# An attention and routed-experts kernel: later loads for step 5, a small table built in three steps, and contiguous one-hots for the large one

## The chip, the cores and the metric

The kernel runs on one core of one Trainium2 chip. The metric is the device time of one execution in microseconds; the time before is 355.25 us, the median of 4 runs (354.03 to 358.31). The engines are named as the profile names them: PE does matrix products (PEld loads their weights), DVE and ACT work element by element, POOL does small work and issues most of the transfers, and SP issues the others.

## The reference

Two layers follow each other. The first is attention with normalized queries and keys; the second sends each token to one of eight experts, by a hash of its token id.

```
q, k, v: (8 batches, 12 heads, 448 tokens, 64)
q_n, k_n = q / rms(q) * g_q, k / rms(k) * g_k          # over the last axis
attn = softmax(q_n @ k_n^T / 8)
x = (attn @ v), transposed to (3584 tokens, 768)
expert = token_ids * 2654435761 % 8
for e in range(8):                                     # w1: (8, 768, 1024), w2: (8, 1024, 768)
    rows = tokens with expert == e
    out[rows] = relu(x[rows] @ w1[e]) @ w2[e]
```

## The kernel before

**Attention** works in 48 steps, each for two heads of a batch that lie six apart; six steps make a batch. A step has these parts: square queries and keys (`prep_sq`, on DVE, or on ACT for the groups in `ACT_SQ`), sum the squares on PE against a unit matrix (`prep_sum`) and finish the sum on DVE (`prep_red`); logarithm and exponential on ACT give the reciprocal root (`prep_ln`, `prep_er`); normalize on DVE (`prep_norm`); transpose on PE and copy out on DVE (`transpose`, `evacuate`); four score products on PE (`score`), four exponentials on ACT (`expo`), the product with the values on PE (`av_part`, in three parts), and the scaling by the row sums on DVE (`row_sums`, `put_x`). The results go to `x_scratch` in DRAM, a batch at a time.

The order is written out by hand: `emit` takes a text of tokens such as `sqk:1.0` (square the keys of group 1), and each engine executes its instructions strictly in the order in which they were emitted. One text covers the setup and the first twelve steps, a second, `steady`, is repeated for batches 2 to 7. `spin:n` emits n matmuls of zeros that keep PE busy. The first steps are loaded singly: step 0 and step 5 (`HP - 1`) from SP and ACT as fp32, the pairs 1 to 2 and 3 to 4 from POOL. The loads of step 5 are issued by SP right behind those of step 0 and of the token ids; the slots of its tiles that no load fills are zeroed by DVE (`zero`, part 3).

**The small table** lists, for experts 0 and 1, which token sits in which slot, so that their rows can be gathered while attention still runs. It is made in pieces between attention steps: small DVE operations stand in `SIDE`, matmuls with a follow-up on DVE in `AV_SIDE`, by the step in which they are placed. The matmuls write into columns of the bank of `av_ps` that attention leaves free; `m13a` does 28 of them at once, one for each column of 128 tokens, in step 31, `m13b` scales the result by -32768 and 1, and `m14a` adds the two halves with a unit matrix (`rep4`) in step 34.

**Experts** work on PE without a break: `gemm1` (48 matmuls, then Relu on ACT or DVE) and `gemm2` for each of four tiles of 128 rows, whose result is copied out by ACT (even tiles) or DVE (odd tiles) and scattered by POOL. Before each tile, `turn` transposes one gathered tile of a later expert on PE into the one bank of `ps_x`, and DVE copies it out. `before` and `between` say which tile is turned where.

**The large table**, for all experts from 2 on, is made while expert 0 runs. `plan` puts its parts behind a group of `gemm1` ("g") or a tile of `gemm2` ("k"). `p3` to `p11` compute each token's slot and split it into a high and a low digit (`hl`). `low` and `high` compare the digits with the numbers 0, 1, 2, ... and so make one-hots; `high_tok` multiplies the high ones by the token number, and `table_mm` takes 28 products of 128 x 56 over them. `fetch(2, ...)` then gathers expert 2's rows. The one-hots are laid out with the digit outside and the 28 columns inside; for that, `numbers` spreads the numbers over a tile `num` on ACT, in four parts.

Of the kernel before, what the change touches and what calls it, by code (L numbers as in the profile page):

```python
# [20 lines left out]
def kernel(  # L21
# [12 lines left out]
    nc = tc.nc  # L34
# [75 lines left out]
    rep4 = consts.tile([P, LO0], FP16)  # L110
# [49 lines left out]
    def setup3():  # L160
# [15 lines left out]
        for g in range(NL):  # L176
            r = slice(LO0 * g, LO0 * g + LO0)
            G.tensor_copy(rep4[r], ident16[r, r])
# [74 lines left out]
    with tc.manual_schedule(), \  # L253
# [96 lines left out]
        ACT_SQ = ((0, 1), (1, 1), (3, 1), (5, 0))  # L350
# [100 lines left out]
        comb = rt([P, 2, 2 * HI0], FP16, "comb")  # L451
# [63 lines left out]
        def m11(e):  # L515
            h = slice(HI0 * e, HI0 * e + HI0)
            V.tensor_tensor(out=hi[:, 1, h], in0=hi[:, 0, h], in1=wide(tv16, HI0), op=ALU.mult)
# [6 lines left out]
        def m13a(av):  # L524
            for c in range(NTC):
                g = LO0 * (c % NL)
                nc.tensor.matmul(av[g:g + LO0, SP:SP + 4 * HI0], lhsT=lo[:, :, c],
                                 rhs=hi[:, :, :, c], start=False, stop=(c >= NTC - NL),
                                 skip_group_check=True)

        def m13b(av):
            for a in range(2):
                o = SP + 2 * HI0 * a
                V.tensor_scalar_mul(comb[:, a], av[:, o:o + 2 * HI0], 1.0 if a else -32768.0)

        def m14a(av):
            for a in range(2):
                nc.tensor.matmul(av[0:LO0, SP:SP + 2 * HI0], lhsT=rep4[:], rhs=comb[:, a],
                                 start=False, stop=(a == 1), skip_group_check=True)
# [10 lines left out]

        def n1():
            V.memset(ones_e[:], 1.0)
# [169 lines left out]
        def zero(part):  # L722
# [11 lines left out]
            elif part == 3:  # L734
                zero_kv(V, raw(1, HP - 1)[:, None])
                zero_q(V, raw(0, HP - 1))
# [11 lines left out]
        load_one(HP - 1)  # L748
# [24 lines left out]
        AV_SIDE = {17: (m5a, m5b), 19: (m7a, m7b), 31: (m13a, m13b), 34: (m14a, m14b)}  # L773
        SIDE = {4: (m1, m2, m3), 5: (m4,), 7: (m8, m9), 11: (n1, n2), 12: (m15,), 13: (n3,),
# [46 lines left out]
        def emit(text, b):  # L821
# [18 lines left out]
            zero:1 zero:6 zero:0 gain:0 sqk:0.0 zero:2 spin:12 sumk:0.0 sqq:0.0 zero:7  # L840
            spin:2 sumq:0.0 redk:0.0 ln:0.1.2 er:0.1.2 redq:0.0 nk:0 ln:0.0.1 zero:3
            spin:3 Tk:0 er:0.0.1 sqk:1.0 spin:1 sumk:1.0 nq:0 sqq:1.0 Tq:0 redk:1.0 kT:0
            sumq:1.0 redq:1.0 qT:0 ln:1 v:1 spin:2 sc:0.0 er:1 nk:1 nq:1 sc:0.1 exp:0.0
            spin:2 Tk:1 kT:1 sc:0.2 kT:2 v:0 sc:0.3 sqk:2.0.0 exp:0.1 exp:0.2 spin:1
            Tq:1 qT:1 av:0.0 qT:2 sc:1.0 exp:0.3 sqk:2.0.1 sc:1.1 sc:1.2 sqq:2.0.0
            sumk:2.0 av:0.1 sqq:2.0.1 exp:1.0 sc:1.3 exp:1.1 redk:2.0 exp:1.2 v:2
            sumq:2.0 redq:2.0 av:0.2 sc:2.0 exp:1.3 ln:2 er:2 sc:2.1 rec:0 sc:2.2 x:0
            exp:2.0 nk:3 av:1.0 nq:3 Tk:3 kT:3 sc:2.3 av:1.1 av:1.2 exp:2.1 kT:4 nk:5
            Tq:3 rec:1 exp:2.2 qT:3 exp:2.3 qT:4 sc:3.0 nq:5 sc:3.1 sqk:3.0 sqq:3.0
            sumk:3.0 redk:3.0 exp:3.0 sc:3.2 exp:3.1 sumq:3.0 sc:3.3 exp:3.2 x:1 av:2.0  # L850
            redq:3.0 ln:3 sqk:4.0 Tk:5 Tq:5 sc:4.0 sc:4.1 exp:3.3 sqq:4.0 av:2.1 er:3
            av:2.2 kT:5 qT:5 sc:4.2 nk:6 exp:4.0 Tk:6 exp:4.1 exp:4.2 sc:4.3 exp:4.3
            sc:5.0 rec:2 x:2 av:3.0 kT:6 kT:7 av:3.1 sumk:4.0 sc:5.1 sc:5.2 nq:6 v:3
            exp:5.0 exp:5.1 redk:4.0 exp:5.2 Tq:6 sqk:4.1 av:3.2 sc:5.3 qT:6 qT:7 rec:3
            x:3 sc:6.0 sumq:4.0 exp:5.3 sc:6.1 sc:6.2 redq:4.0 sumk:4.1 exp:6.0 sqq:4.1
            av:4.0 redk:4.1 sqk:5.0 sc:6.3 sumq:4.1 exp:6.1 exp:6.2 av:4.1 redq:4.1 ln:4
            av:4.2 sc:7.0 sc:7.1 exp:6.3 er:4 sumk:5.0 v:4 rec:4 x:4 nk:8 redk:5.0
            av:5.0 Tk:8 nq:8 kT:8 exp:7.0 av:5.1 kT:9 av:5.2 rec:5 sqq:5.0 x:5 sc:7.2
            sumq:5.0 sc:7.3 exp:7.1 redq:5.0 av:6.0 exp:7.2 Tq:8 av:6.1 av:6.2 exp:7.3
            nk:10 qT:8 sc:8.0 sqq:5.1 sc:8.1 qT:9 exp:8.0 rec:6 x:6 sc:8.2 exp:8.1  # L860
            sumq:5.1 av:7.0 sc:8.3 nq:10 redq:5.1 exp:8.2 Tk:10 sqk:5.1 kT:10 av:7.1
            av:7.2 sc:9.0 exp:8.3 exp:9.0 kT:11 sc:9.1 rec:7 x:7 sc:9.2 Tq:10 exp:9.1
            av:8.0 v:5 qT:10 qT:11 sc:9.3 av:8.1 sumk:5.1 sqq:6.0 exp:9.2 redk:5.1
            exp:9.3 ln:5 av:8.2 er:5 rec:8 sc:10.0 sc:10.1 sc:10.2 x:8 sumq:6.0 exp:10.0
            av:9.0 av:9.1 exp:10.1 nk:14 nk:12 redq:6.0 av:9.2 sc:10.3 nq:12 rec:9 Tk:12
            exp:10.2 x:9 exp:10.3 sc:11.0 sc:11.1 av:10.0 kT:12 kT:13 exp:11.0 av:10.1
            sqq:6.1 Tq:12 qT:12 exp:11.1 sc:11.2 av:10.2 qT:13 rec:10 sc:11.3 nq:14
            exp:11.2 sc:12.0 x:10 sumq:6.1 exp:11.3 exp:12.0 redq:6.1
# [26 lines left out]
    with tc.manual_schedule(), \  # L895
# [108 lines left out]
        num = m_rt.tile([P, P, NTC], FP16)  # L1004
        lo1 = m_rt.tile([P, P, NTC], FP16)
        hi1 = m_rt.tile([P, NHI - HB, NTC], FP16)
# [74 lines left out]
        def numbers(part):  # L1081
            r = slice(32 * part, 32 * part + 32)
            nc.scalar.copy(num[:, r], iota_h[:, r, None].to_broadcast([P, 32, NTC]))
            if part == 3:
                nc.scalar.copy(tvh[:], tv[:])

        def low(part):
            r = slice(32 * part, 32 * part + 32)
            V.tensor_tensor(out=lo1[:, r], in0=num[:, r],
                            in1=hl[:, 1, None, :].to_broadcast([P, 32, NTC]), op=ALU.is_equal)  # L1090

        def high():
            V.tensor_tensor(out=hi1[:], in0=num[:, HB:NHI],
                            in1=hl[:, 0, None, :].to_broadcast([P, NHI - HB, NTC]),
                            op=ALU.is_equal)

        def high_tok():
            V.tensor_tensor(out=hi1[:], in0=hi1[:],
                            in1=tvh[:, None, :].to_broadcast([P, NHI - HB, NTC]), op=ALU.mult)

        def table_mm():
            val = ps_h.tile([P, 512], FP32, name="h_ps")[:, 0:NHI - HB]
            for c in range(NTC):
                nc.tensor.matmul(val, lhsT=lo1[:, :, c], rhs=hi1[:, :, c],
                                 start=(c == 0), stop=(c == NTC - 1))
# [19 lines left out]
        def each(f, *parts):  # L1125
# [3 lines left out]
            (0, "g", 0): each(numbers, 0), (0, "g", 1): [p3] + each(numbers, 1),  # L1129
            (0, "g", 2): [p4, p5] + each(numbers, 2), (0, "g", 3): [p6] + each(numbers, 3),  # L1130
            (0, "g", 4): [p7, p8], (0, "g", 5): [p9, p10, p11],
            (0, "g", 6): each(low, 0, 1), (0, "g", 7): each(low, 2, 3) + [high],
            (0, "k", 0): [high_tok], (0, "k", 1): [table_mm, lambda: fetch(2, range(KT))],
# [89 lines left out]
```

## Time and profile before

| | us |
|---|---|
| median of 4 runs | 355.25 |
| the profiled execution | 356.22 |
| its span, first to last instruction | 354.6 |
| ACT's first square / first exponential | 6.04 / 15.63 |
| matmuls of the small table, step 31 | 119.42 to 121.28 |
| first product of expert 0 | 169.89 |
| matmuls of the large table | 185.00 to 187.86 |
| last scatter | 348.87 |

A row of the timeline gives the start, the length, the engine, the line of the kernel, the operation with its output and input, and how often it stands there; in square brackets stands how long the engine was idle before it, and what ended the wait. A row of the busy times by stage gives a stretch, its length and the busy time of each engine in it.

### The profile page before, as it was taken

The numbers are of one execution on the slowest core, as the hardware profiler recorded it, in microseconds if no ns is written. First come the engines' busy times: TensorE is split into PE (matmuls) and PEld (weight loads), VectorE is DVE, ScalarE is ACT, GpSimd is POOL, SyncE is SP. The second block draws the span as 40 slices with busy tenths as digits, with TensorE's granted clock in tenths as the row PEclk, the third lists the DMA queues.
The fourth block names the chain that finished last, engine by engine and source line by source line (L and its number), as shares of the span: only waits on it lengthen the run. The fifth ranks groups of instructions, "written<-read, shape, count | busy, mean of one in ns | idle before, by whom it ended". The sixth has DMA issues, their size and how long they took to land. (4 is left out here: it accounts for less than half of the span.)

```text
span 354.6 us, 9268 instructions
## 1 busy us (share of the span) xinstructions
PE 335.6 (95%) x3894; PEld 235.2 (66%) x3894; DVE 202.9 (57%) x486; ACT 190.5 (54%) x289; POOL 146.6 (41%) x202
## 2 busy tenths in 40 slices
PE   5989999999999999997999999999999999999992
PEld 2466776766677777664867767767676676766751
DVE  2799999999999799773672243232232233223210
ACT  2499999999999899997722221212111111211210
POOL 8789926325420100012565455736456461303122
PEclk9699999999999999998999999999999999999997
DMA  6999999999999998032589999999999995203012
GB/s 85 209 202 205 199 236 200 238 202 219 203 248 211 252 209 194 3 79 68 130 171 203 272 276 239 258 250 236 260 220 267 228 232 186 112 0 125 24 71 90
DMA packets 41659, 64.82 MB, mean 183 GB/s; under 512 B 9743, under 2 KB 29655, under 8 KB 41232
## 3 DMA queue, kind: packets, MB, share of 16 engines
q0 software_dynamic: 37856, 58.10, 81.8%
q1 hardware_dynamic: 3456, 5.90, 5.4%
q8 instruction: 31, 0.51, 0.5%
q10 hardware_dynamic: 304, 0.21, 0.2%
q14 instruction: 12, 0.10, 0.1%
HBM read 89.29 MB, written 17.30 MB: 301 GB/s over the span
## 5 line engine op out<-in xcount | busy, mean ns | idle before, releaser
L632 ACT ACTIVATE expT<-sc_ps 128x896 bf16<-128x896 f32 x144 | 123.5, 935 | 5.7 <-PE sc_ps L616 5.1
L928 PEld LDWEIGHTS <-h_sb 128*128 128x128 f16 (+1 forms) x512 | 51.2, 104 | 30.5 <-ACT h_sb L915 0.5
L941 POOL DMA_INDIRECT out_dram<-o_sb,gidx x32 | 32.5, 1017 | 83.9 <-ACT o_sb L938 55.0
L928 PE MATMUL o_ps<-w_sb,h_sb 128*128 128x512 f16 (+3 forms) x384 | 66.2, 326 | 0.0
L915 ACT ACTIVATE h_sb<-h_ps 128x480 f16<-128x480 f32 (+2 forms) x44 | 21.7, 498 | 68.7 <-PE h_ps L911 61.9
L911 PEld LDWEIGHTS <-w_sb 128*128 128x128 f16 x336 | 44.5, 146 | 15.6 <-issue 1.2
L220 POOL DMA_INDIRECT kr<-x_scratch,gidx x32 | 32.7, 1022 | 48.0 <-DVE srec L673 37.1
L938 ACT COPY o_sb<-o_ps 128x768 f32<-128x768 f32 x16 | 12.8, 799 | 69.8 <-PE o_ps L928 57.3
L911 PE MATMUL h_ps<-xT,w_sb 128*128 128x480 f16 x240 | 49.4, 366 | 0.0
L650 PE MATMUL av_ps<-v,expT 128*128 128x65 bf16 x864 | 46.0, 194 | 3.0 <-DVE x_sb L681 2.9
L650 PEld LDWEIGHTS <-expT 128*128 128x128 bf16 x864 | 39.4, 98 | 14.0 <-DVE x_sb L681 8.6
L616 PE MATMUL sc_ps<-qT,kT 64*128 64x448 f16 x288 | 44.3, 361 | 1.5 <-DVE qT L608 0.6
L917 DVE TENSOR_SCALAR h_sb<-h_ps 128x480 f16<-128x480 f32 x28 | 18.4, 658 | 47.2 <-PE h_ps L911 47.2
L938 DVE COPY o_sb<-o_ps 128x768 f32<-128x768 f32 (+1 forms) x15 | 14.3, 956 | 33.6 <-PE o_ps L928 33.6
L232 DVE COPY xT<-xT_ps 128x768 f16<-128x768 f16 x28 | 15.5, 553 | 28.7 <-PE xT_ps L231 28.7
L294 POOL DMA_DIRECT2D vr<-in_v_dram x36 | 23.8, 671 | 17.0 <-DMA kr<-in_k_dram 6.2
L681 DVE TENSOR_TENSOR x_sb<-av_ps,srec 128x448 f16<-128x448 f32 x48 | 29.9, 623 | 1.4
L376 PEld LDWEIGHTS <-ident 128*128 128x128 f16 x576 | 23.2, 100 | 10.7 <-issue 5.7
L635 ACT ACTIVATE expT<-sc_ps 128x448 bf16<-128x448 f32 x48 | 27.6, 575 | 0.0
L655 PE MATMUL av_ps<-v,expT 128*128 128x130 bf16 x144 | 25.3, 222 | 0.0
L605 DVE TENSOR_SCALAR kT<-qkT_ps,g_col 128x512 f16<-128x512 f16 x48 | 21.0, 478 | 2.7 <-PE qkT_ps L576 2.5
L928 PE MATMUL o_ps<-kr,h_sb 128*128 128x512 f16 (+3 forms) x128 | 22.1, 326 | 0.0
(202 smaller groups left out, 452.0 us busy)
## 6 DMA issues: line engine op xcount, KB each, us to landing
w_sb<-in_moe_w_dram POOLq DMA_DIRECT2D x18, 512.0 KB
w_sb<-in_moe_w_dram POOLq DMA_DIRECT2D x8, 768.0 KB
kr<-in_k_dram POOLq DMA_DIRECT2D x7, 672.0 KB
qr<-in_q_dram POOLq DMA_DIRECT2D x7, 672.0 KB
x_scratch<-x_sb SPq DMA_DIRECT2D x15, 288.0 KB, 6.7
w_sb<-in_moe_w_dram POOLq DMA_DIRECT2D x2, 1536.0 KB
qr<-in_moe_w_dram POOLq DMA_DIRECT2D x6, 512.0 KB
vr<-in_v_dram POOLq DMA_DIRECT2D x14, 192.0 KB
```

The lines of the kernel that those rows point to most:

```text
L220: nc.gpsimd.indirect_dma_start(out=xg[0:idx.shape[0], :], out_offset=None, in_=x_dram[0:rows, :], in_offset=bass.IndirectOffsetOnAxis(ap=i ...
L294: eng.dma_start(out=dst[64 * half:64 * half + 64, :, s0:s0 + cnt, :].rearrange("p n s d -> p n (s d)"), in_=runs(t, h0 + HP * hh, 1, n, to ...
L616: nc.tensor.matmul(sc[:, hh, :S], lhsT=kT[64 * hh:64 * hh + 64, P * j:P * j + P], rhs=qT[64 * hh:64 * hh + 64, :], start=True, stop=True)
L632: nc.scalar.activation(expT[:, 2 * j:2 * j + 2, :], sc[:, :, :S], AF.Exp, bias=0.0, scale=1.0)
L635: nc.scalar.activation(expT[:, 6, :], sc[:, 0, :S], AF.Exp, bias=0.0, scale=1.0)
L650: nc.tensor.matmul(av[:, 2 * t + hh, :], lhsT=expT[:, tl(hh, j), P * t:P * t + P], rhs=v8[:, i, vs(hh, j), 0:D + 1], start=(hh == 0 and t ...
L655: nc.tensor.matmul(av[:, 2 * t:2 * t + 2, :], lhsT=expT[:, 6, P * t:P * t + P], rhs=v8[:, i, 0::7, 0:D + 1], start=False, stop=False)
L681: nc.vector.tensor_tensor(out=xs[b][:, :, hp * D:hp * D + D], in0=av[:, :, :D], in1=srec[:, :, None].to_broadcast([P, SL, D]), op=ALU.mult)
L911: nc.tensor.matmul(h_ps[:, :c1 - c0], lhsT=w1v[:, co, fo, :], rhs=xT[:, co, c0:c1], start=(co == 0), stop=(co == CO - 1))
L928: nc.tensor.matmul(o_ps[d0 > 0][0:w, d0:d1], lhsT=h_sb[:, fo, col * P:col * P + w], rhs=w2_sb[:, fo, d0:d1], start=(fo == 0), stop=(fo == ...
L938: (nc.vector.tensor_copy if col % 2 else nc.scalar.copy)(o_sb[0:w], o_ps[0][0:w])
L941: scat = nc.gpsimd.indirect_dma_start(out=out[:, :], out_offset=bass.IndirectOffsetOnAxis(ap=idx[0:w], axis=0), in_=o_sb[0:w], in_offset=N ...
```

## The change

Four things change together.

1. **The first steps.** Step 5's loads are no longer emitted at once: `zero` part 3 now emits two ACT copies of zeros into the free slots and the loads behind them, and the order text has it behind the first squares. The square of group 3's keys is no longer in `ACT_SQ`, and goes to DVE. The whole text of the first steps is another one.
2. **The small table.** Its matmuls are split over steps 31, 32 and 33 (10, 10 and 8). Each part is copied out by itself; the scaling by -32768 and 1 moves into the matrix `rep`, so `m14a` does six small matmuls, in step 35. The product of the high one-hots with the token number (`m11`) goes from DVE to POOL. `m15` and `n3` swap places, and `ones_e` is filled by POOL in the setup.
3. **The large table.** The one-hots are laid out with the columns outside and the digit inside, so that the operands of each matmul are contiguous; `numbers` and its tile go. `one_hot` compares the row of numbers, repeated for each column, with each column's digit, repeated for each number.
4. **The plan of expert 0.** `high`, `high_tok`, `table_mm` and `fetch(2)` each stand one tile later; two turned tiles swap places.

```diff
-    rep4 = consts.tile([P, LO0], FP16)
+    rep = consts.tile([P, 2, LO0], FP16)
...
-            G.tensor_copy(rep4[r], ident16[r, r])
+            for a, one in enumerate((-32768.0, 1.0)):
+                G.tensor_scalar(out=rep[r, a], in0=ident16[r, r], scalar1=one, scalar2=None,
+                                op0=ALU.mult)
+        G.memset(ones_e[:], 1.0)
...
-        ACT_SQ = ((0, 1), (1, 1), (3, 1), (5, 0))
+        ACT_SQ = ((0, 1), (1, 1), (5, 0))
...
-        comb = rt([P, 2, 2 * HI0], FP16, "comb")
+        PIECES = 3
+        comb = rt([P, PIECES, 2, 2 * HI0], FP16, "comb")
...
         def m11(e):
             h = slice(HI0 * e, HI0 * e + HI0)
-            V.tensor_tensor(out=hi[:, 1, h], in0=hi[:, 0, h], in1=wide(tv16, HI0), op=ALU.mult)
+            nc.gpsimd.tensor_tensor(out=hi[:, 1, h], in0=hi[:, 0, h], in1=wide(tv16, HI0), op=ALU.mult)
...
-        def m13a(av):
-            for c in range(NTC):
+        def m13a(av, i):
+            c1 = min(10 * i + 10, NTC)
+            for c in range(10 * i, c1):
...
-        def m13b(av):
-            for a in range(2):
-                o = SP + 2 * HI0 * a
-                V.tensor_scalar_mul(comb[:, a], av[:, o:o + 2 * HI0], 1.0 if a else -32768.0)
+        def m13b(av, i):
+            V.tensor_copy(comb[:, i].rearrange("p a h -> p (a h)"), av[:, SP:SP + 4 * HI0])
 
         def m14a(av):
-            for a in range(2):
-                nc.tensor.matmul(av[0:LO0, SP:SP + 2 * HI0], lhsT=rep4[:], rhs=comb[:, a],
-                                 start=False, stop=(a == 1), skip_group_check=True)
+            for i in range(PIECES):
+                for a in range(2):
+                    nc.tensor.matmul(av[0:LO0, SP:SP + 2 * HI0], lhsT=rep[:, a], rhs=comb[:, i, a],
...
             elif part == 3:
-                zero_kv(V, raw(1, HP - 1)[:, None])
-                zero_q(V, raw(0, HP - 1))
+                z = warm[:, 0:4 * D].rearrange("p (s d) -> p s d", d=D)
+                nc.scalar.copy(raw(1, HP - 1)[:, 0::7], z[:, 0:2])
+                nc.scalar.copy(raw(0, HP - 1)[64:P, 3::4], z[64:P, 0:2])
+                load_one(HP - 1)
...
         setup1()
-        load_one(HP - 1)
...
-        AV_SIDE = {17: (m5a, m5b), 19: (m7a, m7b), 31: (m13a, m13b), 34: (m14a, m14b)}
-        SIDE = {4: (m1, m2, m3), 5: (m4,), 7: (m8, m9), 11: (n1, n2), 12: (m15,), 13: (n3,),
+        AV_SIDE = {17: (m5a, m5b), 19: (m7a, m7b), 35: (m14a, m14b)}
+        for i in range(PIECES):
+            AV_SIDE[31 + i] = (lambda av, i=i: m13a(av, i), lambda av, i=i: m13b(av, i))
+        SIDE = {4: (m1, m2, m3), 5: (m4,), 7: (m8, m9), 11: (n2,), 12: (n3,), 13: (m15,),
...
-            zero:1 zero:6 zero:0 gain:0 sqk:0.0 zero:2 spin:12 sumk:0.0 sqq:0.0 zero:7
-            spin:2 sumq:0.0 redk:0.0 ln:0.1.2 er:0.1.2 redq:0.0 nk:0 ln:0.0.1 zero:3
-            spin:3 Tk:0 er:0.0.1 sqk:1.0 spin:1 sumk:1.0 nq:0 sqq:1.0 Tq:0 redk:1.0 kT:0
-            sumq:1.0 redq:1.0 qT:0 ln:1 v:1 spin:2 sc:0.0 er:1 nk:1 nq:1 sc:0.1 exp:0.0
...
+            zero:0 zero:2 zero:7 sqk:0.0 zero:3 sqq:0.0 spin:12 sumk:0.0 spin:2 sumq:0.0
+            zero:1 redk:0.0 ln:0.1.2 zero:6 er:0.1.2 sqk:1.0 nk:0 spin:4 sumk:1.0
+            redq:0.0 ln:0.0.1 sqq:1.0 er:0.0.1 Tk:0 sumq:1.0 nq:0 redk:1.0 gain:0 Tq:0
+            redq:1.0 kT:0 qT:0 spin:3 sc:0.0 ln:1 sc:0.1 sc:0.2 er:1 nk:1 exp:0.0 Tk:1
+            nq:1 exp:0.1 sqk:2.0.0 kT:1 kT:2 exp:0.2 v:0 sqk:2.0.1 sc:0.3 spin:2 Tq:1
...
-        num = m_rt.tile([P, P, NTC], FP16)
-        lo1 = m_rt.tile([P, P, NTC], FP16)
-        hi1 = m_rt.tile([P, NHI - HB, NTC], FP16)
+        lo1 = m_rt.tile([P, NTC, P], FP16)
+        hi1 = m_rt.tile([P, NTC, NHI - HB], FP16)
...
-        def numbers(part):
-            r = slice(32 * part, 32 * part + 32)
-            nc.scalar.copy(num[:, r], iota_h[:, r, None].to_broadcast([P, 32, NTC]))
-            if part == 3:
-                nc.scalar.copy(tvh[:], tv[:])
+        def tok16():
+            nc.scalar.copy(tvh[:], tv[:])
+
+        def one_hot(dst, values, digits):
+            n, w = digits.shape[1], values.shape[1]
+            V.tensor_tensor(out=dst, in0=values[:, None, :].to_broadcast([P, n, w]),
+                            in1=digits[:, :, None].to_broadcast([P, n, w]), op=ALU.is_equal)
 
         def low(part):
-            r = slice(32 * part, 32 * part + 32)
-            V.tensor_tensor(out=lo1[:, r], in0=num[:, r],
-                            in1=hl[:, 1, None, :].to_broadcast([P, 32, NTC]), op=ALU.is_equal)
+            c = slice(NTC // 4 * part, NTC // 4 * (part + 1))
+            one_hot(lo1[:, c], iota_h, hl[:, 1, c])
 
         def high():
-            V.tensor_tensor(out=hi1[:], in0=num[:, HB:NHI],
-                            in1=hl[:, 0, None, :].to_broadcast([P, NHI - HB, NTC]),
-                            op=ALU.is_equal)
+            one_hot(hi1[:], iota_h[:, HB:NHI], hl[:, 0])
 
         def high_tok():
             V.tensor_tensor(out=hi1[:], in0=hi1[:],
-                            in1=tvh[:, None, :].to_broadcast([P, NHI - HB, NTC]), op=ALU.mult)
+                            in1=tvh[:, :, None].to_broadcast([P, NTC, NHI - HB]), op=ALU.mult)
...
-                nc.tensor.matmul(val, lhsT=lo1[:, :, c], rhs=hi1[:, :, c],
+                nc.tensor.matmul(val, lhsT=lo1[:, c], rhs=hi1[:, c],
...
-            (0, "g", 0): each(numbers, 0), (0, "g", 1): [p3] + each(numbers, 1),
-            (0, "g", 2): [p4, p5] + each(numbers, 2), (0, "g", 3): [p6] + each(numbers, 3),
+            (0, "g", 0): [tok16], (0, "g", 1): [p3], (0, "g", 2): [p4, p5], (0, "g", 3): [p6],
             (0, "g", 4): [p7, p8], (0, "g", 5): [p9, p10, p11],
-            (0, "g", 6): each(low, 0, 1), (0, "g", 7): each(low, 2, 3) + [high],
-            (0, "k", 0): [high_tok], (0, "k", 1): [table_mm, lambda: fetch(2, range(KT))],
+            (0, "g", 6): each(low, 0, 1), (0, "g", 7): each(low, 2, 3), (0, "k", 0): [high],
+            (0, "k", 1): [high_tok], (0, "k", 2): [table_mm, lambda: fetch(2, range(KT))],
...
-        before[0, 0], before[0, 1], before[0, 2] = [t(1, 0)], [t(0, KT - 1)], [t(1, 1)]
+        before[0, 0], before[0, 1], before[0, 2] = [t(1, 0)], [t(1, 1)], [t(0, KT - 1)]
```

## The prediction

> **What bounds the kernel now.** I read the page first, then the engines by stage, then three stretches that the change touches in order of time. The chain of waits is no help here: it ends after one scatter.
>
> ```profile
> span 354.6 us, 9268 instructions
> ...
> PE 335.6 (95%) x3894; PEld 235.2 (66%) x3894; DVE 202.9 (57%) x486; ACT 190.5 (54%) x289; POOL 146.6 (41%) x202
> ```
>
> PE's 95% is an average over two very different stages. The busy times by stage (columns: stretch, length, then busy us of PE, PEld, DVE, ACT, POOL, then clock, DMA share, GB/s) show it:
>
> ```profile
> 24.00:30.00 6.00, 5.15 (x94) 3.39 (x91) 5.72 (x14) 5.86 (x11) 5.30 (x20) 1.00 1.42 198
> ...
> 114.00:134.00 20.00, 20.00 (x362) 14.78 (x361) 17.73 (x48) 18.18 (x27) 1.43 (x2) 1.00 1.07 227
> 134.00:152.00 18.00, 17.37 (x299) 11.87 (x299) 15.34 (x40) 18.00 (x27) 0.00 (x0) 1.00 0.35 85
> ```
>
> From 24 to 152 us attention is held by ACT's exponentials (18.00 of 18 us in a batch), with PE so close behind that extra PE work becomes ACT idleness. From 170 us PE alone is the bound (149.2 busy of 150 us from 192 on). Before 15.6 us it is a chain through all engines. So an us saved counts on that chain before 15.6, on ACT up to 168, on PE after it.
>
> **1. The start.** DVE, in order of time:
>
> ```profile
> 8.21 0.21 DVE L186 TENSOR_SCALAR g_col<-gcol 128x1 f32<-128x1 f32 x1 [5.08 <-DMA gcol<-in_g_k_dram]
> 8.49 0.63 DVE L366 TENSOR_TENSOR sq_q<-expT 128x512 f16<-128x512 f32 x1
> 10.42 0.69 DVE L424 TENSOR_TENSOR n_one<-expT,rr 128x512 f16<-128x512 f32 x1 [0.44 <-ACT rr L401]
> 11.74 0.69 DVE L424 TENSOR_TENSOR n_one<-expT,rr 128x512 f16<-128x512 f32 x1
> ```
>
> The first query square stands behind the gain product, which waits 5.08 us for a tiny load. The new order puts the gain after step 1's sums, and moves step 5's three zero memsets (0.11 + 0.11 + 0.17) off DVE to two ACT copies, which fit in ACT's wait between 6.67 and 9.84. The trace has ACT's own square at 6.04, so the query square can run at about 7, and the first key norm at about 8.9 instead of 10.42. But the first query norm, the later one, gains less: the new order puts step 1's key square ahead of the second logarithm on ACT, and step 1's query square ahead of the norm on DVE. Those wait for loads. POOL, which waits for both, shows step 1's keys in by 10.7 and its queries by 11.9. Moving step 5's six loads (448 KB) on SP behind the ACT copies takes away a part of the traffic that competes until then; nothing else stands behind them on SP before the store at 42 us. At the 174 GB/s of 5.3 to 15.6 us, the 110 KB or so of them that land before step 1's are worth 0.6 us, and their new start near 7 us gives half of it back. So the query square comes at 11.3 to 11.4, the norm at about 11.9 against 11.74, and then PE has four groups in line: step 1's key sums, the key transposes, the query sums, the query transposes, 0.95, 0.8, 0.95 and 0.4 us at the half clock that the trace has from 8.7 to 15.5. That puts the first scores at about 15.2 against 15.04 now. Were the clock full there, the same groups and the spins take 1.0 us less. I take **0.0** for the first exponentials, bounds -1.0 to +0.6 (the upper one: step 5's keys late for their square, now at 18.93, with step 1's query copies queued behind it).
>
> **2. ACT's square of group 3's keys** (0.97 us at 25.43) goes to DVE, where the same shape takes 0.62. ACT is full there (5.86 of 6 us), so up to 0.97 goes. DVE is at 5.72 of 6, and from 24 to 42 has 1.1 us free in 18; 0.62 goes in, but not where it is free. **-0.6**, bounds -0.97 and 0.
>
> **3. The small table** in step 31:
>
> ```profile
> 119.42 0.56 ACT L635 ACTIVATE expT<-sc_ps 128x448 bf16<-128x448 f32 x1
> 119.42 1.93 PE L527 MATMUL av_ps<-hi,lo 128*64 128x32 f16 x28
> 121.28 0.36 PE L616 MATMUL sc_ps<-qT,kT 64*128 64x448 f16 x2
> 121.74 0.92 ACT L632 ACTIVATE expT<-sc_ps 128x896 bf16<-128x896 f32 x1 [1.77 <-PE sc_ps L616]
> ```
>
> 28 matmuls at 66 ns (the weights are read with a stride, and stay so) hold the next scores for 1.85 us, and ACT idles 1.77: next to nothing was in hand. It is the one large ACT gap between 20 and 160 us. Split 10, 10, 8, each third holds PE 0.66, 0.66, 0.53 us. How much hides depends on how far scores are ahead: in steps 30 to 47 the first scores of a step end just 0.1 us ahead of their exponential in about half of the steps, 0.25 to 0.6 in most others. So each third loses some 0.2 to 0.3 us less than its length; the six reduction matmuls for two (some 50 ns each, +0.2) and the third copy of 0.17 on DVE take part of that back. Gain between 1.77 and -0.6 (no slack, all additions on the path); I take **-0.4**, nearer to the end that the 0.1 us rows point to.
>
> The token product of the one-hots (two of 0.27 us) moves from DVE to POOL, where the nearest row is 0.42 us for 128x128. It stands in POOL's queue after the last attention loads and ahead of the first expert's weights, issued at 88.62 now, and must wait for DVE's one-hot at 94.5. So those weights start 7 to 8 us later. The DMA engines fall to a share of 0.35 in 134 to 152 us, and the weights are used at 169.9: the delay is hidden. If it were not, it would cost the part of 8 us that exceeds this lull. 0. The index copy and the class counts swap places; the first gather that needs the indices is at 158: 0.
>
> **4. Expert 0.** DVE and PE after 178 us:
>
> ```profile
> 178.43 2.23 DVE L1089 TENSOR_TENSOR lo<-num,hl 128x896 f16<-128x896 f16 x4
> 180.58 0.97 DVE L1093 TENSOR_TENSOR hi<-num,hl 128x1568 f16<-128x1568 f16 x1
> 181.47 0.55 DVE L232 COPY xT<-xT_ps 128x768 f16<-128x768 f16 x1
> 181.93 0.96 DVE L1098 TENSOR_TENSOR hi<-hi,tvh 128x1568 f16<-128x1568 f16 x1
> ...
> 182.07 0.49 PE L231 MATMUL xT_ps<-ident,kr 128*128 128x128 f16 x6 [0.48 <-DVE xT L232]
> 182.40 2.76 PE L928 MATMUL o_ps<-w_sb,h_sb 128*128 128x512 f16 x16
> 185.00 3.04 PE L1104 MATMUL h_ps<-hi,lo 128*128 128x56 f16 x28
> ```
>
> PE: the 28 table matmuls take 104 ns each. Contiguous weights of 128 columns with a like stream (65 columns, L650) go at 32 ns: 2.87 becomes 1.0, **-1.9**. ACT loses four copies of 0.94, so the last Relu comes earlier and a 0.18 stall of the second product goes.
>
> DVE: every one-hot now reads one operand whose innermost step repeats a single element. No two-byte row of the trace does that; all two-byte rows at about half a ns per element (0.62 for 896) read neighbours in both. Bounds: those rows, or the four-byte ones, 0.39 at 224 and 0.66 at 512 elements, that is 0.94 ns more per element: 1.02 at 896, 1.65 at 1568. I take the latter, since only rows without a repeated element have the former. Then the four low parts end at 182.2 instead of 180.6, and behind them waits the copy that frees the only transpose bank: PE, done with the first product at 181.25, waits for 182.8, a stall of 1.55 against 0.65 now. High, the copies and the token product fill DVE to 188.4, and the next bank is free only at 189.0 while PE asks at 187.85: another 1.15. In sum -1.9 - 0.2 + 0.9 + 1.15 = **0.0**, and I put +0.1 for the longer queue. At the lower bound there is a stall of 0.5 in place of both: -2.2. The later gathers for expert 2 start near 192 against 189.2 and are used past 207: hidden.
>
> [...]
>
> **Sum.** 0.0 - 0.6 - 0.4 + 0.1 = -0.9. The profiled execution took 356.22 (span 354.6 and 1.6 around it), so it would be 355.3; it lies 0.97 above the median of the runs shown, 355.25, so on that the forecast is **354.3**.
>
> **Rivals.**
> *Slower: the clock falls behind the new stalls.* In this trace a stretch of 3.4 us in which PE was busy 1.57 (0.46) was followed by one at half clock:
>
> ```profile
> 158.90:162.31 3.41, 1.57 (x23) 0.65 (x18) 0.66 (x3) 1.71 (x3) 2.46 (x3) 1.00 0.42 115
> 162.31:165.73 3.42, 3.08 (x36) 2.01 (x36) 1.05 (x3) 2.75 (x5) 0.00 (x0) 0.50 0.22 62
> ```
>
> 2.70 of 3.42 (0.79, 152.07 to 155.49) had no such effect. With stalls of 1.55 and 1.15 us, the stretches from 179.4 and 186.2 come to 0.55 and 0.66, between the two. If both fall, each costs half of 3.4 us: +3.4, and 354.3 becomes 357.7; with the small table's upper bound 358.7. It decides from a busy share under about 0.6. Against it: 0.46 is the only drop after the start. Chance 0.17.
>
> *Faster: nothing comes in the way.* The one-hots keep half a ns (-2.2), the thirds hide (-1.77), the square's 0.97 goes whole, and the start gains 1.0: -5.9, 349.3. Some two thirds of it is 351.3. For it: ACT has no other gap from 20 to 160 us. Against it: the 0.1 us leads, and a DVE that is busy 5.72 of 6 us. Chance 0.22.
>
> *It does not do what it says:* the thirds give back all 1.77 and the plan's square lands on the critical DVE: 355.3. Chance 0.11. The forecast keeps 0.5, with its own range 353.2 to 355.8.
>
> **How the numbers follow.** Of this kernel 1% is about what a measurement can tell from no change: 351.7 and 358.8. The faster case lies past it for most of its 0.22: 0.20. Of the slower case 0.09 does, and 0.02 of a late step 5: 0.11. The rest, 0.69, is within. The range reaches from 351.0, just under the faster case's 351.3, to 358.2, between the slower one's two prices.
>
> **What would show it.** The gain product no longer ahead of the query square; the first exponential at 15 to 16; the ACT gap of 1.77 replaced by three of 0.2 to 0.6; 28 table matmuls in about 1 us; low parts of 1.0 us; a stall of PE at each of two transposes, and the granted clock there. I would be wrong if the low parts stay at 0.62, if the clock drops near 183, or if step 1's loads land before 10.5.

## The result and the profile after

The changed kernel takes 354.73 us (median of 51 runs, 353.17 to 356.13), the kernel before 355.47 in the runs beside them (78 runs). The ratio is 0.9977, with a 95% interval of 0.9968 to 0.9986: 0.5 to 1.1 us less. 354.3 was forecast. The profiled execution took 355.89 (before: 356.22).

The page of the changed kernel, and its busy times in the stretches shown before (stretch, length, busy us of PE, PEld, DVE, ACT, POOL, clock, DMA share, GB/s):

```profile
span 354.3 us, 9261 instructions
PE 333.0 (94%) x3898; PEld 232.6 (66%) x3898; DVE 206.4 (58%) x482; ACT 188.2 (53%) x286; POOL 149.1 (42%) x207
```

```profile
24.00:30.00 6.00, 5.48 (x102) 3.66 (x99) 5.79 (x16) 5.76 (x10) 5.30 (x20) 1.00 1.42 197
114.00:134.00 20.00, 20.00 (x366) 14.83 (x363) 17.94 (x48) 18.37 (x27) 1.42 (x2) 1.00 1.05 223
134.00:152.00 18.00, 17.49 (x306) 12.06 (x303) 15.30 (x39) 18.00 (x27) 0.00 (x0) 1.00 0.43 99
```

Around the small table ACT is busy 0.19 us more than before, and PE has its 20.00 of 20.00 as before. The timeline of DVE at the start, and of ACT there and at the small table:

```profile
6.51 0.69 DVE L369 TENSOR_TENSOR sq_q<-expT 128x512 f16<-128x512 f32 x1 [3.69 <-DMA expT<-in_q_dram]
...
8.29 0.62 DVE L427 TENSOR_TENSOR n_one<-expT,rr 128x512 f16<-128x512 f32 x1
...
11.24 0.63 DVE L369 TENSOR_TENSOR sq_q<-qr 128x896 f16<-128x896 f16 x1 [2.24 <-DMA qr<-in_q_dram]
11.78 0.69 DVE L427 TENSOR_TENSOR n_one<-expT,rr 128x512 f16<-128x512 f32 x1
```

```profile
14.82 2.54 ACT L634 ACTIVATE expT<-sc_ps 128x896 bf16<-128x896 f32 x3 [1.19 <-PE sc_ps L618]
...
119.78 0.92 ACT L634 ACTIVATE expT<-sc_ps 128x896 bf16<-128x896 f32 x1 [0.66 <-PE sc_ps L618]
...
126.87 2.54 ACT L634 ACTIVATE expT<-sc_ps 128x896 bf16<-128x896 f32 x3 [0.60 <-PE sc_ps L618]
```

The first norm moved to 8.29 (8.9 was worked out) and the second stayed at 11.78 (11.9); the first exponential came at 14.82, not at 15.6. The gap of 1.77 at the small table became 0.66, 0.12 (at 123.10) and 0.60. In expert 0, DVE and PE:

```profile
177.25 4.10 DVE L1090 TENSOR_TENSOR lo<-iota_h,hl 128x896 f16<-128x896 f16 x4
...
181.73 1.78 DVE L1090 TENSOR_TENSOR hi<-iota_h,hl 128x1568 f16<-128x1568 f16 x1
...
185.87 1.78 DVE L1101 TENSOR_TENSOR hi<-hi,tvh 128x1568 f16<-128x1568 f16 x1
...
197.81 0.56 DVE L235 COPY xT<-xT_ps 128x768 f16<-128x768 f16 x1 [6.65 <-remote]
```

```profile
181.87 0.49 PE L234 MATMUL xT_ps<-ident,kr 128*128 128x128 f16 x6 [1.76 <-DVE xT L235]
...
188.18 0.49 PE L234 MATMUL xT_ps<-ident,kr 128*128 128x128 f16 x6 [1.15 <-DVE xT_e L235]
...
189.38 0.89 PE L1107 MATMUL h_ps<-hi,lo 128*128 128x56 f16 x28
...
194.12 0.50 PE L234 MATMUL xT_ps<-ident,kr 128*128 128x128 f16 x6
...
196.69 1.29 PE L933 MATMUL o_ps<-w_sb,h_sb 128*96 128x512 f16 x9 [0.36 <-ACT h_sb L920]
198.43 0.77 PE L916 MATMUL h_ps<-xT,w_sb 128*128 128x480 f16 x3 [0.45 <-DVE xT L235]
```

A low part takes 1.02 us, the 28 matmuls 0.7 from the first start to the last, and the two stalls at the transposes are there. New are the two stalls behind the table: PE transposed at 194.12, but DVE copied the result out only at 197.81; "remote" says that the profile names no engine of this core for the end of that wait.

The two traces alone mislead in one point. The first exponential is 0.8 us earlier, expert 0 begins 1.1 us earlier (168.77 for 169.89) and at expert 1 only 0.1 is left (198.43 for 198.52). That reads as "all of the gain is the start, and the table costs 1 us". The experiments say otherwise.

### The profile page after: what moved, and what is told of

It is laid out like the page before. It is cut to its first block, busy times and chain, and to the rows that moved or that the text cites. A ratio compares the mean times of both kernels' runs of the same rounds, so it can differ in the third digit from the quotient of the medians.

```text
span 354.3 us, 9261 instructions
## 1 busy us (share of the span) xinstructions
PE 333.0 (94%) x3898; PEld 232.6 (66%) x3898; DVE 206.4 (58%) x482; ACT 188.2 (53%) x286; POOL 149.1 (42%) x207
## 5 line engine op out<-in xcount | busy, mean ns | idle before, releaser
L946 POOL DMA_INDIRECT out_dram<-o_sb,gidx x32 | 33.7, 1054 | 85.0 <-ACT o_sb L943 55.6
L916 PEld LDWEIGHTS <-w_sb 128*128 128x128 f16 x336 | 44.4, 146 | 15.6 <-issue 1.3
L943 ACT COPY o_sb<-o_ps 128x768 f32<-128x768 f32 x16 | 12.8, 798 | 69.8 <-PE o_ps L933 59.1
L235 DVE COPY xT<-xT_ps 128x768 f16<-128x768 f16 x28 | 15.5, 553 | 29.8 <-PE xT_ps L234 23.1
L379 PEld LDWEIGHTS <-ident 128*128 128x128 f16 x576 | 22.4, 98 | 11.1 <-issue 6.8
```

Source lines behind the costliest of these rows:

```text
L916: nc.tensor.matmul(h_ps[:, :c1 - c0], lhsT=w1v[:, co, fo, :], rhs=xT[:, co, c0:c1], start=(co == 0), stop=(co == CO - 1))
L943: (nc.vector.tensor_copy if col % 2 else nc.scalar.copy)(o_sb[0:w], o_ps[0][0:w])
L946: scat = nc.gpsimd.indirect_dma_start(out=out[:, :], out_offset=bass.IndirectOffsetOnAxis(ap=idx[0:w], axis=0), in_=o_sb[0:w], in_offset=N ...
```

## The experiments

Each kernel is compared with runs of the kernel before on its own chip; the numbers behind its name are that ratio, its 95% interval and the median time. The changed kernel was not run again in these groups, so a difference to it goes through two ratios, and some tenths of a us can't be told that way. Three marks from the traces serve for comparing: the first exponential of step 13 (59.56 us before), the way from there to step 45 (97.60), and the time from expert 0's first product to expert 1's first full one (28.62).

**e1: the first steps undone.**

```
+ order text, load_one(HP - 1), zero part 3 and ACT_SQ of the kernel before
```

> The changed kernel with its first steps put back: the order text of the first twelve steps, the early loads of step 5 with their zeros on DVE, and the square of group 3's keys on ACT, all as before; small table, large table and plan as changed. The recorded sum has the start at 0.0 and the square at -0.6 us, so undoing both gives the changed kernel's time + 0.6 (355.3), with the first exponential about where the changed kernel has it (14.8 us) or up to 0.4 us from it. The rival, read from the two traces: the clock stays full one stretch longer with the new order, which is worth 0.8 us, and the square nothing: first exponential back at 15.6 us, half clock from 8.7 us on, time + 0.8 (355.5), and the steps from 13 on late by the same 0.8 as the first exponential.

1.0028 (1.0008 to 1.0047), 356.15 us. First exponential at 15.54, half clock from 8.60 to 15.42, step 13 at 59.44. Against the changed kernel's trace (58.92) the first steps, with the square, are worth 0.5 us, against its ratio 0.8 to 2.8 us; the recorded terms had 0.6. The two causes aren't told apart yet.

**e2: the square on ACT again, in the new order; e9: the square on DVE, in the old order.**

```
e2 -        ACT_SQ = ((0, 1), (1, 1), (5, 0))
   +        ACT_SQ = ((0, 1), (1, 1), (3, 1), (5, 0))
e9 the reverse, in the kernel before
```

> The changed kernel with one entry put back: the square of group 3's keys runs on ACT again (0.97 us there) and not on DVE (0.62 us); order text unchanged. Recorded term: ACT is full in those steps, so this costs 0.6 us (bounds 0 and 0.97): 355.3, and the exponentials from step 4 on come 0.6 us later than in the changed kernel. The rival: in these steps PE and DVE are as full as ACT, and the exponentials wait for the scores anyway, so putting it back costs 0 to 0.2 us and the idle time of ACT between steps 2 and 12 shrinks by about 0.9 us.

> The kernel before with one entry changed: the square of group 3's keys on DVE (0.62 us) and no longer on ACT (0.97 us); its order text and all else stay. Recorded term: -0.6 us (bounds -0.97 and 0), so the first exponential of step 13 comes at 58.9 us (59.4 to 59.6 in the three traces with the old order and ACT's square) and the median is 0.6 below the kernel before (354.5 to 354.6). The rival, from the run that put the square back into the new order and lost 1.4 to 2.0 us: the new order is worth nothing without this entry and the entry nothing without the order, since in the old order the square then stands in DVE's queue ahead of step 3's sums: step 13 at 59.4 to 59.6 and the time as before (355.1).

e2: 1.0035 (1.0014 to 1.0056), 356.42 us, step 13 at 60.97. e9: 1.0029 (1.0002 to 1.0056), 357.52 us beside 356.25, step 13 at 61.02. With both halves, step 13 comes at 59.1 (mean of nine traces, 58.53 to 59.50); three traces with the old order and ACT's square have 59.37, 59.44 and 59.56. So each half alone is 1.5 us or more late, but not for the same reason. For e9 it shows in ACT's timeline of the kernel before, which the prediction had not shown, beside that of e9:

```profile
25.43 0.97 ACT L364 ACTIVATE sq_k<-kr 128x896 f16<-128x896 f16 x1
26.54 1.73 ACT L632 ACTIVATE expT<-sc_ps 128x896 bf16<-128x896 f32 x2
```

```profile
26.47 1.73 ACT L632 ACTIVATE expT<-sc_ps 128x896 bf16<-128x896 f32 x2 [0.98 <-PE sc_ps L616]
28.51 0.92 ACT L632 ACTIVATE expT<-sc_ps 128x896 bf16<-128x896 f32 x1 [0.32 <-PE sc_ps L616]
...
30.55 1.73 ACT L632 ACTIVATE expT<-sc_ps 128x896 bf16<-128x896 f32 x2 [0.32 <-PE sc_ps L616]
```

In the old order the square filled a wait for scores: without it, ACT stands idle for 0.98 us and the exponential starts at the same time. DVE, which now makes the square at 26.82 ahead of the queries' one, is later with everything behind it, and further waits open. Up to here e9 is level with the kernel before; the 1.5 us are lost behind the square.

For e2 it is another matter. ACT in the changed kernel, then two stretches of e2 and ACT behind them:

```profile
22.10 2.77 ACT L634 ACTIVATE expT<-sc_ps 128x896 bf16<-128x896 f32 x3
```

```profile
10.53:13.94 3.41, 2.71 (x42) 2.45 (x42) 1.69 (x5) 1.13 (x4) 2.92 (x5) 0.50 1.37 217
13.94:17.36 3.42, 3.42 (x19) 1.43 (x18) 2.39 (x5) 2.20 (x5) 1.79 (x3) 0.50 1.32 221
```

```profile
23.42 2.71 ACT L634 ACTIVATE expT<-sc_ps 128x896 bf16<-128x896 f32 x3
26.03 0.94 ACT L367 ACTIVATE sq_k<-kr 128x896 f16<-128x896 f16 x1
```

Up to its square e2 is the same program as the changed kernel, and its trace is late already: step 2 begins at 23.42, in the nine traces at 21.21 to 22.37. Two stretches at half clock lie ahead of it, where the nine have one or none. From step 2 to step 13 e2 takes 37.55 us, the nine 36.82 to 37.32 (mean 37.11). So in the new order ACT's square costs some 0.4 of the 1.9 us in this trace, near the 0.6 of the recorded term; in the old order taking it away costs 1.5.

**e8: the gain product alone; e5: more spins.**

```
e8 -            zero:1 zero:6 zero:0 gain:0 sqk:0.0 ...     (kernel before)
   +            zero:1 zero:6 zero:0 sqk:0.0 ...  Tq:0 redk:1.0 gain:0 kT:0
e5 -            ... sqk:1.0 nk:0 spin:4 sumk:1.0            (changed kernel)
   +            ... sqk:1.0 nk:0 spin:12 sumk:1.0
```

> The kernel before with a single token of its order text moved: the gain product, which waits for a small load until 8.2 us, stands behind step 1's key sums and no longer ahead of the first query square. The recorded working: the query square comes forward by 1.5 us and the first key norm with it, but behind them step 1's sums and transposes follow each other as before, so the first exponential stays (15.6 us) and so does the time. The rival: the query sums fill PE in the stretch from 5.3 to 8.7 us, the clock stays full more often, and the first exponential is at 14.6 to 15.0, the time 0.5 to 0.8 us below the one before, without the later loads of step 5.

> The changed kernel with 12 instead of 4 matmuls of zeros ahead of step 1's key sums, in a stretch in which PE otherwise idles 1.8 to 2.5 us. Nothing is queued behind them that could start earlier, so if PE's order alone sets the start, nothing changes (354.7). Theory of the clock: the grant is decided stretch by stretch of 3.41 us, on a grid whose offset differs from execution to execution, by how busy PE was in the stretch before; in the five traces of the old and new order the offset alone decides whether none, one or two stretches of the start are at half clock. With PE filled in, none of them should be, whatever the offset: full clock until about 162 us, first exponential at 13.7 to 14.3 us (14.8, 15.7, 14.9 and 13.7 us in the four traces with the new order, with 1, 2, 1 and 0 stretches at half clock), and a median 0.3 to 0.8 us below the changed kernel's (354.0 to 354.4).

e8: 1.0002 (0.9983 to 1.0021), 355.27 us. First exponential at 14.40, 1.2 us earlier; step 13 at 59.37, 0.1 to 0.2 earlier. e5: 1.0013 (0.9991 to 1.0036), 355.93 us. The clock stays full, as the theory of the clock had it:

```profile
4.52:7.93 3.41, 2.38 (x41) 1.49 (x40) 1.22 (x5) 1.63 (x5) 3.41 (x7) 1.00 0.92 85
7.93:11.35 3.42, 2.24 (x18) 1.11 (x16) 1.03 (x4) 1.14 (x2) 2.04 (x3) 1.00 1.19 182
11.35:14.76 3.41, 3.10 (x54) 1.89 (x52) 3.28 (x9) 1.23 (x4) 3.22 (x5) 1.00 1.30 227
```

The first exponential is at 14.31, but ACT then waits 1.31 us ahead of step 1 (0.82 in the changed kernel), and step 13 is at 59.24, in the middle of the others. So neither the earlier first exponential nor a full clock in place of one stretch at half clock is worth anything by step 13; both theories of the start's 0.8 us fall. What step 13 does go with is the landing of step 1's keys: in eight traces with both halves of the change and four spins, step 13 comes 48.8 to 49.3 us behind the square of these keys (9.34 to 10.29 us), whether none or one stretch was at half clock. That the landing is the cause is argued, not shown: no run moves it alone. And a second stretch at half clock may well count: in e2's trace, the only one of this order that has two, step 2 is 13.2 us behind this square, in these eight 11.9 to 12.2. That e5's runs are slower than the changed kernel's isn't explained; at 161.5 to 168.4 us its trace has two stretches at half clock, but so has e3's, whose runs are not slower; the others have one or none.

**e3: the small table in one piece.**

```
-        PIECES = 3                              c1 = min(10 * i + 10, NTC)
+        PIECES = 1                              c1 = NTC
```

> The changed kernel with the small table's 28 matmuls in one piece in step 31 again, one copy and two reduction matmuls (in step 35). Recorded term: the split is worth 0.4 us (bounds 1.77 and -0.6), so the time is + 0.4 (355.1), one ACT gap of about 1.8 us near 120 us in place of three of 0.66, 0.12 and 0.60, and the exponentials from step 36 to the end of attention are 0.4 us later than in the changed kernel. The rival: the split only spreads the same matmuls, and the gain that is seen at step 33 is given back by step 36: less than 0.15 us at step 36 and in the time.

1.0005 (0.9987 to 1.0024), 355.18 us. The gap of 1.77 us is back, at 120.96, and yet step 36 follows step 30 after 19.59 us (changed kernel: 19.62), and step 45 follows step 13 after 97.55 (97.53). The split is worth nothing in the trace. The ratios put it at 1.0 us (1.0005 against 0.9977, intervals that almost touch), but by the same reckoning e1, e3 and e4 would give up 1.8, 1.0 and 0.4 us, 3.2 in all, where the whole change is worth 0.8; no stretch from step 13 to step 45 shows it. If e3 stands for the changed kernel in its group (e1 to e4, one chip), e1 is 1.0 us slower than it, e2 1.2, and e4 as fast (355.13 for 355.18). In these 20 us PE has no free time: the 28 matmuls cost PE the same in three pieces (a median of 294 ns each in the kernel before and in the changed one), and ACT waits that much, once or in small pieces. That PE sets the pace is argued from its 20.00 of 20.00; that the split doesn't matter by step 45 is shown in one trace.

**e4: the large table and its plan undone.**

```
+ num, numbers(), lo1/hi1 with the columns inside, plan and before[0, ...] of the kernel before
```

Undone is part 4 of the sum, the large table with the plan of expert 0; the start and the small table stay as changed.

> [...] The recorded sum has this part at +0.1 us, so the time is that of the changed kernel within 0.2 us (354.6). The rival, read from the traces: the part costs 1.0 us (stalls of PE of 1.76, 1.15 and, beyond the table, 0.36 and 0.45 us, against 2.1 us saved in the 28 matmuls), so undoing it gives -1.0: 353.7, with the first full product of expert 1 1.0 us earlier behind the first product of expert 0 (28.6 us, not 29.7). If the late stalls of 0.36 and 0.45 us belong to the one profiled execution and not to the change, it is -0.3 (354.4).

0.9989 (0.9970 to 1.0008), 355.13 us: by the ratios 0.4 us slower than the changed kernel, with intervals that overlap, and as fast as e3. Either is near the recorded sum's term (+0.1 for the part, so -0.1 for undoing it) and far from the gain of 1.0 us that the two first traces had suggested. Expert 0 takes 29.28 us here, not 28.62, and the clock falls behind the table:

```profile
183.34:186.75 3.41, 3.41 (x36) 3.38 (x34) 0.96 (x1) 0.00 (x0) 1.11 (x2) 1.00 1.06 223
186.75:190.16 3.41, 3.41 (x14) 1.49 (x12) 1.24 (x5) 0.00 (x0) 1.90 (x2) 0.50 0.97 183
```

The stretch that holds the old table counts as 3.41 us busy of 3.41, and yet half clock follows. A matmul of 56 columns every 104 ns counts as busy but streams little. Counted by columns, with the 480 per 202 ns of the long products as full (48 of them take 9.88 us in e7's rows below, the last one 0.37 of it), that stretch is 0.35 full. e9 has the same (half clock from 189.40). In the kernel before, the border between two stretches fell into its table, and nothing happened. So the old table takes 28.62 us at best, and 29.28, 29.40 and 30.67 in e4, e9 and e8 (there a half-clock stretch and a stall of 0.93 behind the table); the changed one takes 28.28, 29.00, 29.06, 29.66 and 29.71, with no half clock. The means are 29.5 and 29.1, closer than the traces of either kind are to each other.

**e7: the gathers of expert 2 later.**

```
-            (0, "k", 2): [table_mm, lambda: fetch(2, range(KT))],
+            (0, "k", 2): [table_mm], (0, "k", 3): [lambda: fetch(2, range(KT))],
```

> The changed kernel with expert 2's four gathers one tile later on POOL, behind the scatter of expert 0's last tile; PE, ACT and DVE unchanged. In three of four traces with the changed table, ACT and DVE took up finished products of PE 0.7 to 3.2 us late, behind the table, and PE then stood still for 0.3 to 0.8 us; each time POOL was at its third and fourth gather. If the gathers do that, the stalls of 0.34 to 0.81 us ahead of expert 1's first full product go, and with them 0.3 to 0.6 us of the time (354.3). If it is the table's place alone, they stay. Should the gathers then be too late for their transposes (from 208 us on), PE waits there instead.

1.0088 (1.0062 to 1.0114), 358.94 us. Expert 0 is down to 27.36 us: behind the table no stall is left. But PE pays for it later:

```profile
190.09 3.25 PE L916 MATMUL h_ps<-xT_e,w_sb 128*128 128x96 f16 x48
193.18 0.50 PE L234 MATMUL xT_ps<-ident,kr 128*128 128x128 f16 x6
193.51 2.76 PE L933 MATMUL o_ps<-w_sb,h_sb 128*96 128x512 f16 x16
196.11 9.88 PE L916 MATMUL h_ps<-xT,w_sb 128*128 128x480 f16 x48
209.32 0.51 PE L234 MATMUL xT_ps<-ident,kr 128*128 128x128 f16 x6 [3.33 <-DMA kr<-x_scratch,gidx]
```

The prediction had booked later gathers as hidden, used past 207. At 192 they are; 7 us later PE waits 3.33, a half-clock stretch follows at 210.48, and the kernel is 4 us slower.

**e6: each digit written twice; e10: the same with the plan of before.**

```
-        hl = m_rt.tile([P, 2, NTC], FP16)
+        hl = m_rt.tile([P, 2, NTC, 2], FP16)          # tvh too
...
-            V.tensor_tensor(out=dst, in0=values[:, None, :].to_broadcast([P, n, w]),
-                            in1=digits[:, :, None].to_broadcast([P, n, w]), op=ALU.is_equal)
+            V.tensor_tensor(out=pairs(dst),            # "p n (u t) -> p n u t", t=2
+                in0=values.rearrange("p (u t) -> p u t", t=2)[:, None].to_broadcast([P, n, w // 2, 2]),
+                in1=digits[:, :, None, :].to_broadcast([P, n, w // 2, 2]), op=ALU.is_equal)
```

> The changed kernel with each digit and token number written twice, side by side, so that the one-hots of the large table are made by operands whose innermost step covers two neighbours; same layout of the result, same matmuls, same plan. The recorded working took 1.02 us for a low part because one operand repeats a single element, and half a ns per element (0.62 us) as the lower bound, at which part 4 would be -2.2 instead of +0.1. If the repeated single element is the reason, the low parts are 0.62 us, the high one and its product 0.97, PE's two stalls of 1.3 to 1.8 and 1.15 us shrink to one of about 0.5, the first product of expert 0 and the first full one of expert 1 are 2.0 to 2.4 us closer (26.3 to 27.5 us; the four traces with the changed table have 28.3 to 29.7), and the time is 352.5. If something else in the new layout slows DVE, the low parts stay at 1.02 and nothing changes.

> The kernel with neighbouring digits (e6), with the parts of the large table and the gathers behind it at the places that they had before, one tile earlier. In e6's trace PE still stands 0.34 us behind the product of the one-hots and the token numbers, and the gathers of expert 2 run at 188.9 to 196.5 us, beside the narrow products in which PE and ACT wait for each other. If the place matters, as in the changed kernel's late stalls, PE's stalls after the table go (0.46 us in e6) and the one ahead of the transposes grows by no more than that: between e6's time and 0.5 below it. If the plan's later place was needed to keep the one-hots off PE's path, a stall of 0.4 to 0.5 us ahead of a transpose comes back, as in the kernel before: e6's time within 0.3.

e6: 0.9906 (0.9881 to 0.9932), 352.23 us beside 355.09. e10: 0.9913 (0.9881 to 0.9945), 352.67 beside 356.25. DVE and PE of e6:

```profile
176.81 2.23 DVE L1093 TENSOR_TENSOR lo<-iota_h,hl 128x896 f16<-128x896 f16 x4
...
179.43 0.96 DVE L1093 TENSOR_TENSOR hi<-iota_h,hl 128x1568 f16<-128x1568 f16 x1
```

```profile
185.05 0.49 PE L234 MATMUL xT_ps<-ident,kr 128*128 128x128 f16 x6 [0.34 <-DVE xT_e L235]
...
186.26 0.89 PE L1113 MATMUL h_ps<-hi,lo 128*128 128x56 f16 x28
```

The repeated single element was the reason for 1.02 us. With pairs, a low part takes 0.62 us in the same layout, of the stalls at the transposes 0.34 is left, and expert 0 takes 25.62 us (e10: 26.32, the plan makes no difference that can be measured). This is the version that beats both kernels; its interval lies clear of the changed kernel's.

**e11 and e12: gathers apart.**

```
             if NS - 4 <= s < NS - 5 + KT:            # in e6
                 c = s - NS + 4
+                if c == 1:
+                    for _ in range(2):               # e12: once
+                        nc.gpsimd.memset(lo[:], 0.0)
```

> The kernel with neighbouring digits (e6), with two memsets of POOL (some 3 us, of a tile that is no longer read) between the first and the second of the three gathers that it issues at 157.5 to 161.2 us, near the end of attention. In nearly all traces, of the kernel before too, ACT and DVE take up scores there 1.7 us late, PE then idles for 2 us and one or two stretches of half clock follow. If the gathers that follow each other on POOL hold these signals up, as the gathers of expert 2 seem to do behind the large table, the wait of 1.7 us at 161 us goes or moves to 163 to 165 us. If it stays at 161 us at its length, the second and third gather are not its cause. The time is e6's less up to 1.7 us, or, where the last gather comes too late for its transposes, more by what these wait.

> As e11, with one memset (1.6 us) between the first and the second of the three gathers. In e11 the wait of 1.7 us at 161 us was gone (the first exponentials of the last three steps came 1.5 to 2.5 us earlier), but PE then waited 1.6 us in all for the two late gathers to land, and expert 0 began when it does in e6. If the gathers hold PE's signals up, the hold falls a little behind its place in e6, some of it into exponentials that are queued, and the gathers land 1.6 us earlier than in e11: expert 0 begins 0.5 to 1.2 us before e6's 168.3 us, and the time is 351.3 to 351.9. If the gap of 1.6 us is too short to matter, the wait of 1.7 us at 161 us is back, and the time is e6's (352.2 to 352.7).

e11: 0.9920 (0.9896 to 0.9944), 353.18 us beside 356.25. ACT's timeline of e10, from the same chip, and of e11:

```profile
159.42 0.56 ACT L637 ACTIVATE expT<-sc_ps 128x448 bf16<-128x448 f32 x1
161.77 1.73 ACT L634 ACTIVATE expT<-sc_ps 128x896 bf16<-128x896 f32 x2 [1.79 <-PE sc_ps L618]
```

```profile
159.13 0.56 ACT L637 ACTIVATE expT<-sc_ps 128x448 bf16<-128x448 f32 x1
159.56 2.57 ACT L634 ACTIVATE expT<-sc_ps 128x896 bf16<-128x896 f32 x3
...
167.41 0.80 ACT L235 COPY xT_e<-sc_ps 128x768 f16<-128x768 f16 x1 [1.66 <-PE sc_ps L234]
```

The wait of 1.79 us is gone, and 1.66 are lost later, with PE waiting 0.70 and 0.93 us for the late gathers: no gain in time. e12: 0.9951 (0.9933 to 0.9969), 350.37 us beside 351.84. No wait at 161 us, and expert 0 begins at 166.86, not 168.30. But on that chip the kernel before itself took 3.3 to 4.4 us less than on the others, so whether the memset or the chip made the wait go isn't settled, and e12 can't be ranked against e6.

## Why the prediction was right in sum, and where it was wrong

The sum was -0.9 us; the runs say -0.5 to -1.1. By the means of the traces it is -0.36 up to step 13, -0.09 from there to step 45 and -0.35 in expert 0, -0.8 in all. This split is no more than an outline: the -0.35 is smaller than the spread of expert 0 in either kernel, and the way from step 45 to expert 0, which the sum leaves out, takes 11.8 to 13.5 us (longest in e3 and e5, with two stretches at half clock there) with a mean of 12.5 in either order. One term of the prediction, the small table, was not there, and one, expert 0, isn't settled; that the total came out so near is in part luck.

**1, the start (0.0).** Right by step 13, wrong for the first exponential, for which it was written: 13.7 to 15.1 us in the traces with both halves of the change, not 15.6 (e2, with two stretches at half clock, has 15.66). The failing step is "the half clock that the trace has from 8.7 to 15.5": the grid of stretches has another offset from one execution to the next (a border at 8.71 us in the kernel before, at 8.80 in the changed one, at 7.93 in e5), and the query square's matmuls now fall ahead of the wait for step 1's keys. The square at 11.24 and the norm at 11.78 were right. That step 1's keys would land no earlier than 10.5 was wrong: their square began at 9.3 to 10.3.

**2, the square (-0.6).** Start and square together came to -0.36 by step 13; in the new order the square's part is some 0.4 (e2's trace from step 2 on, one trace). The size was about right, the reason was not. "ACT is full there (5.86 of 6 us), so up to 0.97 goes" is read from the kernel before, and there it took a busy engine for a late one: the square filled a wait for scores, and its move alone costs 1.5 us (e9). Something is saved only in the new order.

**3, the small table (-0.4).** Measured -0.09, none of it by the split (e3's trace). The failing step is the bound: the row that the prediction itself showed had PE busy 20.00 of 20.00 us, and a gap on ACT beside a full PE is not a gain in hand.

**4, expert 0 (+0.1).** The mechanism was right: 1.02 for a low part (forecast 1.02), 1.78 for the high one (1.65), stalls of 1.3 to 1.8 (1.55) and 1.15 (1.15), the table down by 2.1 (1.9). Two things were missed, of opposite sign: the late signals behind the table, 0.3 to 0.8 us in four of five traces, and the half clock that the old table brings in some executions. What they leave of the +0.1 isn't settled: -0.35 by the means of the traces, -0.4 by the ratios, nothing beside e3.

**The rivals.** The slower one, a clock that falls behind the new stalls, did not come in any of the five traces with them. In the changed kernel's trace, the two stretches in question were 1.66 of 3.42 and 2.26 of 3.41 us busy, and full clock followed both. The "about 0.6" was an estimate between the 0.46 and 0.79 of the trace before; 1.66 of 3.42 is 0.49. The clock fell behind the table that was taken away. The faster one did not come either: its largest part, half a ns per element, isn't in the changed kernel. In e6, which has it, the kernel is at 352.2, between the forecast and that rival's 351.3.

## What to carry to other kernels

Before work is taken from a full engine, look at what stands ahead of the next instruction that matters: the square that filled ACT's wait of 0.98 us cost nothing in the old order (e9), where moving it cost 1.5 us, and in the new order moving it paid some 0.4. Where two engines are full, ask whether the other has time to fill a gap on the one: splitting up the 1.77 us on ACT, beside PE's 20.00 of 20.00 us, brought 0.02 us from step 13 to step 45 (e3's trace). Compare parts of a change within one group of runs that holds the whole change too, or parts of some tenths can't be told. An operand that repeats one element slowed DVE's 2-byte work here from 0.62 to 1.02 us for 896 elements; writing that element twice, side by side, gave it back, and that was worth some 2.5 us of 355 (e6 against the changed kernel, by their ratios).

## What the runs showed of the hardware

**Which clock follows goes with the columns streamed, not with the busy time.** In 14 traces the clock changes only on a grid of 3.41 us, whose offset to the kernel differs from execution to execution (borders at 8.71 us in the kernel before, 8.80 in the changed one, 7.93 in e5). Counted by columns as above, up to 340 us all stretches that were less than 0.39 full (23 or 24, by how a product across a border is counted) were followed by half clock, none that was 0.54 or more was, and between the two both occur. Busy time, by which e5's theory of the clock went, does not part them: 3.41 of 3.41 us were followed by half clock in e4, 1.66 of 3.42 by full clock in the changed kernel. The mean granted clock of the runs is 0.990 for the changed kernel, and 0.983 to 0.984 for the one before on the chips of e1 to e11.

**Gathers from POOL go with late signals of PE.** Beside several indirect gathers in a row, ACT and DVE took up finished products of PE 0.7 to 3.2 us late (3.2 in the changed kernel, whose transposes of 194.12 end at 194.62 and are copied at 197.81), at 161 us in the kernel before too (ACT's wait there: 1.70). With the gathers moved, the delay went from its place, in e7 and in e11; in e3 and e6 it didn't come behind the table. What holds the signals up remains open.

**One chip ran the kernel before in 351.84 us, the others in 355.1 to 356.3.** Times are compared only within a chip here; whether a ratio carries over from one chip to another no run shows.
